# Summary-key copies on three engines instead of GpSimd, longer filler matmuls, and a new order of work in a fused attention and MLP kernel

## The chip, the cores and the metric

The kernel runs on one core of a Trainium2 chip. A core has five engines with an instruction stream each: TensorE (PE, matrix products; its weight loads are shown apart as PEld), VectorE (DVE), ScalarE (ACT), GpSimd (POOL) and SyncE (SP), which here only starts transfers (DMAs). Each engine works through its stream in order and waits at an instruction until the semaphores that it names have come. The metric is the device time of one execution in microseconds (us), less being better.

## The reference

```
scores_l = scale * q @ k^T             # only |i - j| < 16 is kept
scores_s = scale * q @ k_sum^T + log(32)
a        = softmax([scores_l, scores_s])
x        = a @ [v, v_sum]
h        = x @ w_in
out      = (h * erf(softplus(h))) @ w_out
```

q, k and v have 4 batches, 8 heads, 768 tokens and 64 features. A summary is made of each block of 32 tokens: k_sum holds the maximum of its 32 keys by feature, v_sum the mean of its values. So each head of a batch has 24 summary keys and 24 summary values. The attention's result, 3072 tokens by 512 features, goes through a gated MLP with 2048 inner features. Everything is float32.

## The kernel before

**Tiling.** The 3072 tokens are taken in six chunks of 512, the 8 heads in four pairs. A chunk and a pair make a *quad* (24 in all): scores, softmax and values for 512 tokens of two heads. A chunk's MLP is done in four groups of 512 inner features, which makes 24 *periods*. The tokens of a chunk are eight blocks of 64; each block needs the 96 keys around it (the window) and the 24 summary keys of its batch. So the tile of keys, `kw` (128 partitions x 8 blocks x 120), has 96 columns per block that a DMA brings from `k_win` (L522), and 24 that are copied from the tile `ksum` of block maxima (L527). Chunks of 512 tokens and batches of 768 don't coincide: a chunk that spans two batches has two such copies, of four blocks each, the others one of eight. Summary values stand in `vw` below 96 rows of window values.

**The first stage.** Chunk 0 takes another way. Its keys and queries (`kf` L484, `qf` L485) come whole, its values (`vt`, two transfers, L489) are summed on PE by products with a selecting matrix (L501), the result `vs` is copied to `vsum` (L504), and from there into the values' tile `vwf`: for pair 0 by an engine (L507), for pairs 1 to 3 by a DMA (L509). Window values come by L492. The weights `rw` (L313) arrive in eight parts and are converted on DVE (L330, L333, L336, then the rest by L352) and ACT (the cast, in the helper at L277). Scores are products at L565, on top of a mask (L556, L557); then row maxima on DVE (L600), the exponentials on ACT (L606), a reciprocal (L618), the normalisation (L622 on DVE or L625 on ACT), transposes on PE (L636), the copy of them on ACT (L641) and the product with the values (L662, tile `px`), which is split into `xh` (L277) and `xl` (L678) for the MLP's first product (L765, tile `h`).

**After it.** From quad 4 on, the keys of the next batch come as `rows` (L443), DVE takes the maxima (L451) and the copies at L527 bring them into `kw`. The MLP goes on with softplus (L783), erf (L884), the gate's products (L891, L896 and L903 on DVE) and the second product (L916 for the first two periods, then L920). From period 8 on, the first product is made at L806.

**What sets the order.** All work is first recorded as a list of operations with the engines that may do each and a cost for each. `P.order` then places them one after the other: it takes the engine that can start first, and on it, of the ready operations, the one with the lowest key. An operation that may go to several engines goes to the one on which it would end first. The table `TUNE` (one entry for each of 2071 operations) shifts the key, and can fix the engine. The stream of each engine is written in the order that comes out. Transfers are streamed by SP in that order too; from the ninth on, an issue is made when the transfer eight before it has landed. `FILL` names operations of PE ahead of which so many filler matmuls stand (`busy`, L959: zeros times zeros into a bank that nobody reads), and `WARM` is their number ahead of everything.

Of the kernel before, what the change touches and what calls it, by code (L numbers as in the profile page):

```python
# [26 lines left out]
NB = T // 64  # L27
NI = NB // 2
NT = T // 128
NS = 24  # L30
LW = 96
NK = LW + NS
# [7 lines left out]
WARM = 14  # L40
# [6 lines left out]
FILL = {40: 3, 51: 17, 60: 8, 90: 3, 108: 3}  # L47
# [132 lines left out]
def bfloat16(x):  # L180

    n = np.array([x], np.float32).view(np.uint32)
    return float(((n + 0x8000) & 0xFFFF0000).astype(np.uint32).view(np.float32)[0])
# [3 lines left out]
def block_attention_mlp(ctx: ExitStack, tc: tile.TileContext, q_t, k_nat, k_win, v_tok, v_nat, v_win, w_in, w_out, out):  # L187
    nc = tc.nc
# [7 lines left out]
    def sb(shape, dtype, name, tag=None):  # L196

        n = math.prod(shape[1:])
        if n % 128 == 0:
            return pool.tile(shape, dtype, name=name, tag=tag or name)  # L200
        t = pool.tile([128, -(-n // 128) * 128], dtype, name=name, tag=tag or name)[0:shape[0], 0:n]
        return t if len(shape) == 2 else t.rearrange("p (a b) -> p a b", a=shape[1]) if len(shape) == 3 else t.rearrange("p (a b c) -> p a b c", a=shape[1], b=shape[2])

    def ps(name, tag):
        return psum.tile([128, 512], F32, name=name, tag=tag)
# [5 lines left out]
    zeros = sb([128, 256], BF16, "zeros")  # L211
# [22 lines left out]
    for i in range(3):  # L234
        c = bfloat16(rest)
# [18 lines left out]
    ksum = sb([128, 2, NP, NS], F32, "ksum")  # L254
    vrows = [slice(LW, NK), slice(0, NS)]
    vsum = sb([NK, NP, 128], F32, "vsum")
# [7 lines left out]
    def pe(us, fn, r=(), w=(), **kw):  # L264
        return P.add({"PE": us}, lambda e: fn(), r, w, **kw)

    def on(us, fn, r=(), w=(), **kw):
        return P.add(us, lambda e: fn(engines[e]), r, w, **kw)

    def act(us, fn, r=(), w=(), **kw):  # L270
        return P.add({"ACT": us}, lambda e: fn(), r, w, **kw)

    def dma(kb, fn, r=(), w=(), hold=2.0, **kw):
        return P.add({"SP": max(0.45, kb / 350.0)}, lambda e: fn(), r, w, hold=hold, **kw)

    def copy(e, o, i):
        e.copy(o, i) if e is nc.scalar else e.tensor_copy(o, i)  # L277
# [194 lines left out]
    st = {}  # L472

    def where(qd):

        ch, p = divmod(qd, NP)
        seqs = {}
        for j in range(NB):
            seqs.setdefault((NB * ch + j) // SB, []).append(j)
        return ch, p, [(b, slice(js[0], js[-1] + 1)) for b, js in seqs.items()]  # L480
# [16 lines left out]
    def vsum_first(bank):  # L497
        def go(t):
            if t == 0:
                tiles[bank] = ps("vs", bank)  # L500
            nc.tensor.matmul(tiles[bank][0:NK], lhsT=pick[:, 20 - 4 * t:140 - 4 * t], rhs=vts[t // 3][:, t % 3], start=(t == 0), stop=(t == 5))  # L501
        for t in range(6):
            pe(0.87, lambda t=t: go(t), [f"vt{t // 3}"], [bank])
        act(0.5, lambda: nc.scalar.copy(vsum[LW:NK], tiles[bank][LW:NK].rearrange("s (p c) -> s p c", p=NP)), [bank], [f"vsum0{p}" for p in range(NP)])  # L504
        for p in range(NP):
            if p == 0:
                on({"POOL": 1.1}, lambda e: e.tensor_copy(st[0]["vw"][LW:NK], vsum[LW:NK, 0:1, :].to_broadcast([NS, NB, 128])), ["vsum00"], ["vwg0"])  # L507
            else:
                dma(100, lambda p=p: nc.sync.dma_start(out=st[p]["vw"][LW:NK], in_=vsum[LW:NK, p:p + 1, :].to_broadcast([NS, NB, 128])), [f"vsum0{p}"], [f"vwg{p}"])  # L509


    def load_quad(qd):
        ch, p, seqs = where(qd)
        s = st[qd] = {}

        def go_q():
            s["qb"] = sb([128, T], F32, "qb")
            nc.sync.dma_start(out=s["qb"], in_=q_t[ch, p])

        def go_k():  # L520
            s["kw"] = sb([128, NB, NK], F32, "kw")
            nc.sync.dma_start(out=s["kw"], in_=k_win[ch, p])  # L522
        dma(262, go_q, w=["qb"])
        dma(465, go_k, w=["kw"])
        for b, js in seqs:
            n = js.stop - js.start
            on({"POOL": 0.1 + 0.05 * n}, lambda e, b=b, js=js, n=n: e.tensor_copy(s["kw"][:, js, LW:NK], ksum[:, b % 2, p:p + 1, :].to_broadcast([128, n, NS])),  # L527
               [f"ksum{b % 2}{p}"], ["kw"])
# [425 lines left out]
    idle = ps("idle", "o3")  # L954

    def busy(n):

        for _ in range(n):
            nc.tensor.matmul(idle[:, 0:256], lhsT=zeros[:, 0:128], rhs=zeros, start=True, stop=True)  # L959

    busy(WARM)

    for p in range(NP):
# [6 lines left out]
    for p in range(3):  # L970
        ksum_first(p)
        scores(p, banks[p])
        softmax(p, banks[p])
    vsum_first("o2")
    ksum_first(3)
    scores(3, banks[3])
# [44 lines left out]
    def follow(n, bank=None):  # L1021
        sums(n, bank)
        load_quad(n)
        with_quad(load_nat, n + 1)
# [12 lines left out]
    for k in range(NPER):  # L1037
# [27 lines left out]
        elif k < FAST:  # L1065
# [21 lines left out]
            if qs + 1 < NQ:  # L1087
                load_quad(qs + 1)
            if qs < NQ:
                load_quad_v(qs)  # L1090
        else:
# [25 lines left out]
            if qs + 1 < NQ:  # L1117
                load_quad(qs + 1)
# [38 lines left out]
    free = {"PE": 4.15, "DVE": 1.4, "ACT": 4.2, "POOL": 5.2, "SP": 0.7}  # L1157
    plan = P.order(free, lambda n: 60 if n < 330 else 0, TUNE, "exp")
    sets = {"exp": "exp_and_others", "log": "natural_log_exp_and_others", "sig": "sigmoid_and_others", "soft": "softplus"}
    filling = True  # L1160
    for o in plan:
        if o["on"] == "PE":
            filling = filling and "o3" not in o["w"]
            if filling:
                busy(FILL.get(o["n"], 0))
        if "load" in o:
            nc.scalar.preload_act_table_set(sets[o["load"]])  # L1167
        o["fn"](o["on"])
# [40 lines left out]
```

## Time and profile before

| | |
|---|---|
| median of 3 runs | 627.41 us (626.2 to 627.84) |
| the profiled execution | 628.78 us |
| its span, first to last instruction | 627.0 us |
| mean granted clock of TensorE | 0.997 |
| PE, DVE, ACT, POOL busy | 614.3, 439.8, 412.8, 47.7 us |
| key copies on POOL (L527) | 28, 19.5 us together |
| filler matmuls on PE (L959) | 48, 7.7 us together |

A row of the profile's timeline gives start, duration, engine, line, operation, the tile written, the tile read, sizes and count; brackets at its end give the idle time of that engine ahead of it, and what ended it. A row of waits gives the total, the number of times and the longest. A row of windows gives the stretch, its length, the busy time and count of PE, PEld, DVE, ACT and POOL, the clock that TensorE was granted (1.00 is full), the share of DMA engines that were busy and the GB/s. A row of groups gives line, engine, operation, tiles and count, then the time together, the mean of one in ns, and the idle time ahead of them. Matmuls overlap, so their durations add up to more than the time from one start to the next.

### The profile page before, as it was taken

How to read it: one execution, taken by the hardware profiler on the slowest of the kernel's cores; microseconds unless marked ns; L12 is line 12 of the kernel's file. 1: busy time of each engine (PE TensorE's matmuls, PEld its weight loads, DVE VectorE, ACT ScalarE, POOL GpSimd, SP SyncE). 2: the span in 40 equal slices, each digit the busy share in tenths (PEclk: the TensorE clock that was granted, in tenths of full speed). 3: DMA queues.
4: the chain of work that ended last, by engine and by line, in shares of the span. 5: the costliest groups of instructions: out<-in, count | busy, mean ns of one | idle time of the engine just before them, and what ended most of it. 6: DMA issues, size and time to landing. Idle time of an engine off the chain costs nothing.

```text
span 627.0 us, 11997 instructions
## 1 busy us (share of the span) xinstructions
PE 614.3 (98%) x4808; PEld 517.9 (83%) x4808; DVE 439.8 (70%) x631; ACT 412.8 (66%) x822; POOL 47.7 (8%) x72
## 2 busy tenths in 40 slices
PE   7799999999999999999999999999999999999997
PEld 4685666888878889888899899898898898899886
DVE  4799999966899897768658657658657576425442
ACT  4579969977869886784585674565766555552550
POOL 2102001000442500000000000000000000000000
PEclk9899999999999999999999999999999999999999
DMA  8988867564767869899857776766597555574621
GB/s 323 266 277 333 275 214 258 190 210 149 274 190 261 313 239 363 294 326 291 289 203 246 280 265 214 247 235 216 223 292 247 197 183 192 202 264 151 253 72 67
DMA packets 36843, 150.23 MB, mean 240 GB/s; under 512 B 3956, under 2 KB 9396, under 8 KB 24244
## 3 DMA queue, kind: packets, MB, share of 16 engines
q1 hardware_dynamic: 36212, 148.95, 69.4%
q8 instruction: 38, 0.62, 0.4%
q10 hardware_dynamic: 576, 0.52, 0.3%
q14 instruction: 17, 0.14, 0.1%
HBM read 124.13 MB, written 23.07 MB: 235 GB/s over the span
## 4 chain that ended last, share of the span: by engine, by line
PE 82%; DMA 7%; ACT 5%; DVE 4%; issue 1%; SPq 1%; POOL 1%; DVEq 0%
PE ops L920 34%; PE hb L806 13%; PE h L765 11%; PE ha L806 10%; PE ops L916 4%; PE px L662 3%; DMA kf<-k_nat 2%; PE pA L565 2%; DMA out<-rows 2%; ACT L1167 2%; DMA rows<-k_nat 1%; PE pA L636 1%; PE pB L636 1%; DMA rows<-v_nat 1%; DVE a L336 1%
## 5 line engine op out<-in xcount | busy, mean ns | idle before, releaser
L920 PE MATMUL ops<-w,gh 128*128 128x512 f32 x704 | 232.1, 395 | 0.0
L920 PEld LDWEIGHTS ops<-w,gh 128*128 128x128 f32 x704 | 132.6, 188 | 27.6 <-issue 0.5
L920 PE MATMUL ops<-w,gl 128*128 128x512 f32 x352 | 137.5, 391 | 0.3 <-DVE gl L903 0.3
L1167 ACT ACT_TABLE_LOAD x86 | 110.3, 1283 | 1.5
L896 DVE TENSOR_TENSOR hc<-wt,hc 128x1024 f32<-128x1024 f32 x44 | 54.9, 1256 | 68.9 <-ACT wt L884 68.9
L765 PE MATMUL h<-xh,w 128*128 128x512 f32 x256 | 89.3, 407 | 0.0
L277 ACT COPY hc<-hb 128x256 f32<-128x256 f32 x50 | 18.6, 373 | 98.7 <-DVE hc L859 37.0
L920 PEld LDWEIGHTS ops<-w,gl 128*128 128x128 f32 x352 | 66.3, 188 | 12.7 <-DVE gl L903 0.7
L606 ACT ACTIVATE pr<-pr,stats 128x120 f32<-128x120 f32 x160 | 61.0, 383 | 7.7 <-DVE stats L615 7.5
L765 PEld LDWEIGHTS h<-xh,w 128*128 128x128 f32 x256 | 48.4, 189 | 12.7 <-issue 1.7
L806 PE MATMUL hb<-w,ws 128*128 128x256 f32 x384 | 56.5, 283 | 0.8 <-DVE hc L277 0.8
L903 DVE TENSOR_TENSOR gl<-hc,gh 128x1024 fp32r<-128x1024 f32 x44 | 54.8, 1244 | 2.0 <-ACT gh L277 1.1
L806 PEld LDWEIGHTS hb<-w,ws 128*128 128x128 f32 x384 | 50.7, 192 | 1.0 <-DVE hc L277 1.0
L884 ACT ACTIVATE wt<-wt 128x1024 f32<-128x1024 f32 x48 | 50.6, 1062 | 0.4
L765 PE MATMUL h<-xl,w 128*128 128x512 f32 x128 | 50.2, 392 | 0.0
L527 POOL COPY kw<-ksum 128x96 f32<-128x96 f32 (+1 forms) x28 | 19.5, 710 | 391.1 <-DMA kw<-k_win 278.3
L277 DVE CAST gh<-hc 128x1024 fp32r<-128x1024 f32 x39 | 28.2, 724 | 15.8 <-PE ops L920 14.2
L872 ACT ACTIVATE wt<-hc 128x1024 f32<-128x1024 f32 x32 | 32.2, 1051 | 0.2
L277 DVE COPY hc<-hb 128x256 f32<-128x256 f32 x46 | 19.4, 423 | 16.4 <-PE hb L806 15.3
L856 DVE TENSOR_TENSOR hc<-hb,hc 128x256 f32<-128x256 f32 x32 | 13.5, 422 | 23.8 <-PE hb L806 22.0
L606 ACT ACTIVATION_READ_ACCUMULATOR pr<-pr,stats 128x1 f32 x160 | 30.0, 187 | 0.0
L916 PE MATMUL ops<-a32s,gw 128*128 128x512 f32 x64 | 29.4, 596 | 0.0
(163 smaller groups left out, 1084.1 us busy)
## 6 DMA issues: line engine op xcount, KB each, us to landing
w<-dr SPq DMA_DIRECT2D x36, 1024.0 KB, 6.8
ws<-ds SPq DMA_DIRECT2D x30, 1024.0 KB, 8.1
kw<-k_win SPq DMA_DIRECT2D x20, 480.0 KB, 5.3
rw<-w_in SPq DMA_DIRECT2D x8, 1024.0 KB, 7.4
rw<-w_out SPq DMA_DIRECT2D x8, 1024.0 KB, 5.2
dr<-w SPq DMA_DIRECT2D x8, 1024.0 KB
ds<-ws SPq DMA_DIRECT2D x8, 1024.0 KB, 6.6
vw<-v_win SPq DMA_DIRECT2D x20, 384.0 KB, 5.2
```

The source lines that it names most:

```text
L277: e.copy(o, i) if e is nc.scalar else e.tensor_copy(o, i)
L527: on({"POOL": 0.1 + 0.05 * n}, lambda e, b=b, js=js, n=n: e.tensor_copy(s["kw"][:, js, LW:NK], ksum[:, b % 2, p:p + 1, :].to_broadcast([12 ...
L606: nc.scalar.activation(s["pr"][:, j], s["pr"][:, j] if qd >= MQ else s["sc"][j // NI][:, i * NK:(i + 1) * NK], AF.Exp, scale=0.125, bias=s ...
L765: nc.tensor.matmul(hs[k, f][:, 0:T], lhsT=w[m], rhs=xt[ch, cc][x], start=(cc == 0 and n == 0), stop=(cc == 3 and n == 2))
L806: nc.tensor.matmul(shape, lhsT=w[m], rhs=y[l], start=first and c == 0 and i == 0, stop=c == 1 and i == 2, skip_group_check=True)
L872: nc.scalar.activation(wt[k, n], hc[k, n], AF.Softplus)
L884: act(0.96, lambda n=n: nc.scalar.activation(wt[k, n], wt[k, n], AF.Erf, scale=-1.0 if k < SOFT else 1.0), [s], [s], table=("sig",), after ...
L896: e.tensor_tensor(hc[k, n], wt.pop((k, n)), hc[k, n], op=ALU.mult)
L903: e.tensor_tensor(gs[k, n][1], hc.pop((k, n)), f32(gs[k, n][0]), op=ALU.subtract)
L916: nc.tensor.matmul(os_[ch, t], lhsT=x[0][:, i % 2, t * 128:(t + 1) * 128], rhs=w32["o", g, i // 2][:, i % 2], start=first, stop=last)
L920: nc.tensor.matmul(os_[ch, t], lhsT=x[y][:, i % 2, t * 128:(t + 1) * 128], rhs=w[m], start=first and n == 0, stop=last and n == 2)
L1167: nc.scalar.preload_act_table_set(sets[o["load"]])
```

## The change

The two copies may now go to three engines, by a helper that issues the copy of whichever engine is chosen; GpSimd's cost in the planner is raised. A filler matmul has 512 columns instead of 256; their number falls from 48 to 33, at other places. The table `TUNE` is a new one throughout (three of its entries are shown).

```
-WARM = 14
+WARM = 7
...
-TUNE = {0: (-3981.299057, 1.5, 0, None), 1: (-3981.726255, 1.5, 0, None), 2: (-3976.161371, 1.5, 0, None), ...
-FILL = {40: 3, 51: 17, 60: 8, 90: 3, 108: 3}
+TUNE = {0: (-4728.546832, 1.5, 0, None), 1: (-4728.985158, 1.5, 0, None), 2: (-4669.297502, 1.5, 0, None), ...
+FILL = {30: 10, 40: 3, 60: 6, 89: 2, 91: 1, 101: 1, 110: 2, 111: 1}
...
             if p == 0:
-                on({"POOL": 1.1}, lambda e: e.tensor_copy(st[0]["vw"][LW:NK], vsum[LW:NK, 0:1, :].to_broadcast([NS, NB, 128])), ["vsum00"], ["vwg0"])
+                on({"POOL": 1.35, "DVE": 1.13, "ACT": 0.95}, lambda e: copy(e, st[0]["vw"][LW:NK], vsum[LW:NK, 0:1, :].to_broadcast([NS, NB, 128])), ["vsum00"], ["vwg0"])
...
-            on({"POOL": 0.1 + 0.05 * n}, lambda e, b=b, js=js, n=n: e.tensor_copy(s["kw"][:, js, LW:NK], ksum[:, b % 2, p:p + 1, :].to_broadcast([128, n, NS])),
+            on({"POOL": 0.5 + 0.05 * n, "DVE": 0.06 + 0.025 * n, "ACT": 0.2 + 0.018 * n}, lambda e, b=b, js=js, n=n: copy(e, s["kw"][:, js, LW:NK], ksum[:, b % 2, p:p + 1, :].to_broadcast([128, n, NS])),
...
     def busy(n):
...
-            nc.tensor.matmul(idle[:, 0:256], lhsT=zeros[:, 0:128], rhs=zeros, start=True, stop=True)
+            nc.tensor.matmul(idle.rearrange("q (n c) -> q n c", n=2), lhsT=zeros[:, 0:128], rhs=zeros.unsqueeze(1).to_broadcast([128, 2, 256]), start=True, stop=True)
```

What becomes of it in the streams is shown at three places. A copy by the helper stands at L277, whichever engine makes it. The first place is the head of SP's stream, the first transfers of the program (vt: values of chunk 0; kf, qf: its keys and queries; rw: weights). Before:

```order
L484 DMA kf<-k_nat 128x768
L485 DMA qf<-q_t 128x512
L489 DMA vt<-v_tok 128x3x512
L313 DMA rw<-w_in 128x2048
L489 DMA vt<-v_tok 128x3x512
L484 DMA kf<-k_nat 128x768
L485 DMA qf<-q_t 128x512 x3
L484 DMA kf<-k_nat 128x768
L492 DMA vwf<-v_win 96x1024
L484 DMA kf<-k_nat 128x768
```

And now:

```order
L485 DMA qf<-q_t 128x512
L484 DMA kf<-k_nat 128x768
L489 DMA vt<-v_tok 128x3x512 x2
L484 DMA kf<-k_nat 128x768
L313 DMA rw<-w_in 128x2048
L485 DMA qf<-q_t 128x512 x3
L484 DMA kf<-k_nat 128x768
L492 DMA vwf<-v_win 96x1024
L484 DMA kf<-k_nat 128x768
```

The second transfer of values and the second of keys have gone ahead of the first part of the weights; the third transfer of keys has the same transfers ahead of it as before. On PE the six products of L501, three before and three behind 17 fillers, now stand together, with ten fillers behind them.

The second place is ACT's stream ahead of the first softplus of the MLP (L783), where h of the first period is copied and the keys of quad 4, the second chunk's first, are made ready. Before:

```order
L641 COPY ptr<-pA 120x512
L641 COPY ptr<-pB 120x512
L277 CAST xh<-px 128x512
L277 CAST w<-a_592 128x1024
L277 COPY hc<-h 128x512 x2
L1167 ACT_TABLE_LOAD
L783 ACTIVATE wt<-hc 128x1024
```

And now:

```order
L641 COPY ptr<-pA 120x512
L641 COPY ptr<-pB 120x512
L277 CAST xh<-px 128x512
L277 CAST w<-a_584 128x1024
L277 COPY hc<-h 128x512
L277 COPY kw<-ksum 128x4x24
L277 COPY hc<-h 128x512
L1167 ACT_TABLE_LOAD
L783 ACTIVATE wt<-hc 128x1024
```

One of quad 4's two key copies, that for the four blocks of batch 0, has come in between the two copies of h. The other, for the four blocks of batch 1, needs the maxima of L451. It stands first of the key copies in GpSimd's stream, which the difference of the two streams behind the constants shows:

```order
-L507 COPY vwf<-vsum 24x1024
-L527 COPY kw<-ksum 128x4x24 x8
-L527 COPY kw<-ksum 128x8x24 x3
+L277 COPY vwf<-vsum 24x1024
+L277 COPY kw<-ksum 128x4x24 x4
+L277 COPY kw<-ksum 128x8x24
 L394 TENSOR_TENSOR sums<-w 128x2x256 x4
```

The copy of the first values has stayed on GpSimd (L507 is L277 now), and seven of 28 key copies have, five of them ahead of the sums of L394; of the others twelve are on ACT and nine on DVE. On DVE, L451 is followed by L333, L352 and L336 as before, and then by a copy of h.

2 lines of the change are left out of this document (1 added, 1 removed).

## The prediction

> **What bounds the kernel now.** I read the page first, then the waits of the engine that is busiest, then those stretches of its timeline in which it waits.
>
> ```profile
> span 627.0 us, 11997 instructions
> PE 614.3 (98%) x4808; PEld 517.9 (83%) x4808; DVE 439.8 (70%) x631; ACT 412.8 (66%) x822; POOL 47.7 (8%) x72
> PE   7799999999999999999999999999999999999997
> PEclk9899999999999999999999999999999999999999
> ```
>
> PE is busy for 614.3 of 627.0 us, and of the 40 slices only the first two and the last lie below 9. So a change that leaves the products as they are can win only what PE loses to waits, to filler matmuls and to a halved clock. The waits of PE, longest first (total, times, longest):
>
> ```profile
> PE vs L501 <- DMA vt<-v_tok: 2.2, 1, 2.2
> PE h L565 <- issue: 2.1, 1, 2.1
> PE pA L565 <- POOL kw L527: 1.6, 1, 1.6
> PE o L565 <- DMA kf<-k_nat: 1.1, 1, 1.1
> PE idle L959 <- DVE zeros L212: 1.1, 1, 1.1
> PE hb L806 <- DVE hc L277: 0.8, 1, 0.8
> PE ops L920 <- DVE gl L903: 0.3, 1, 0.3
> ```
>
> One of the seven is for a copy of summary keys: 1.6 us. The last two (1.1 us) are all that PE waits after 52 us, up to its last product, so everything else lies in the first stage, where the timeline of PE (start, duration, count, idle before) shows it:
>
> ```profile
> 9.35 2.81 PE L501 MATMUL vs<-vt,pick 128*120 128x512 f32 x6 [2.22 <-DMA vt<-v_tok]
> 11.99 2.02 PE L959 MATMUL idle<-zeros 128*128 128x256 bf16 x17
> 13.85 2.80 PE L501 MATMUL vs<-vt,pick 128*120 128x512 f32 x6
> 18.85 0.49 PE L959 MATMUL idle<-zeros 128*128 128x256 bf16 x3
> 20.45 0.97 PE L565 MATMUL o<-kf,qf 64*64 64x16 f32 x36 [1.11 <-DMA kf<-k_nat]
> 23.18 1.05 PE L959 MATMUL idle<-zeros 128*128 128x256 bf16 x8
> 27.73 0.30 PE L565 MATMUL h<-kf,qf 64*64 64x96 f32 x2 [2.11 <-issue]
> 34.44 0.49 PE L959 MATMUL idle<-zeros 128*128 128x256 bf16 x3
> 50.51 0.31 PE L565 MATMUL pA<-kw,qb 64*64 64x120 f32 x1 [1.56 <-POOL kw L527]
> 51.08 0.50 PE L765 MATMUL h<-xh,w 128*128 128x512 f32 x1
> 56.68 3.59 PE L916 MATMUL ops<-a32s,gw 128*128 128x512 f32 x8
> ```
>
> A filler takes (13.85 - 11.99) / 17 = 0.109 us. The 2.11 us pause waits for no data. The transfers of 25 to 26 us contain one packet of instructions, and I read the pause as PE running out of code while its next block stands behind data:
>
> ```profile
> q8 instruction: 1, 0.02, 7.4%
> 24.56:27.97 3.41, 1.30 (x51) 1.03 (x52) 1.89 (x3) 2.91 (x17) 0.00 (x0) 1.00 1.01 344
> 27.97:31.38 3.41, 3.41 (x43) 3.23 (x37) 2.60 (x7) 1.03 (x3) 0.00 (x0) 0.50 1.05 223
> 7.49:10.90 3.41, 1.55 (x4) 0.83 (x5) 0.50 (x2) 2.78 (x16) 0.00 (x0) 1.00 1.01 374
> ```
>
> The last three rows are stretches of 3.41 us (first PE, last but two the granted clock). After the one with 1.30 us of PE work the clock is 0.50 for the whole next one, which costs half of it, 1.7 us. The one with 1.55 us of work had no such follower (the page's second slice, 15.7 to 31.4 us, is the only one after the first below 9 tenths). So a point between 1.30 and 1.55 us of work decides here. The Trainium skill, "TensorE: Matmul & The Clock Gate", Part 1, says that the clock drops after an idle window of about 3.4 us; by that rule a pause of 2.1 us inside a window would cost nothing, and then the term for the clock below would be no gain of the change at all. The row with 0.50 contradicts it here, and the measurement decides.
>
> What really sets the start of the second quad's chain is not PE but VectorE and GpSimd:
>
> ```profile
> 28.78 1.22 DVE L600 TENSOR_REDUCE stats<-h 128x4 f32<-128x480 f32 x2 [2.29 <-PE h L565]
> 33.64 0.69 DVE L277 CAST xh<-px 128x512 fp32r<-128x512 f32 x1 [0.56 <-PE px L662]
> 45.99 0.94 DVE L451 TENSOR_REDUCE ksum<-rows 128x24 f32<-128x768 f32 x1
> 46.85 1.21 DVE L333 SCALAR_TENSOR_TENSOR a32s<-rw,a32s 128x1024 uint32<-128x1024 uint32 x1
> 49.12 1.22 DVE L336 SCALAR_TENSOR_TENSOR a32s<-rw,a32s 128x1024 uint32<-128x1024 uint32 x1
> 45.00 0.26 POOL L527 COPY kw<-ksum 128x96 f32<-128x96 f32 x1 [25.69 <-DVE a L336]
> 46.99 3.47 POOL L527 COPY kw<-ksum 128x96 f32<-128x96 f32 x1 [1.73 <-DVE ksum L451]
> ```
>
> DVE has no gap from 28.78 on but the 0.56 us before 33.64. Then L451 makes the maxima, and the copy of them, which took 0.26 us when alone, takes 3.47 us: it ends at 50.46, just after the last of the three weight conversions of DVE (L333, L352, L336) that began with it. PE starts 0.05 us later. So the first-stage pause of PE pushes DVE, and DVE pushes that copy and PE.
>
> **The change part by part.** *The copies.* Of 28 key copies twelve go to ACT, nine to DVE, and seven stay on GpSimd, among them the one that PE waits for. The copy of the first values stays there too. Their prices come from these groups (busy, mean ns, idle before; in the row of k_win issues, KB each and us to landing; the last two rows are of the timeline):
>
> ```profile
> L527 POOL COPY kw<-ksum 128x96 f32<-128x96 f32 (+1 forms) x28 | 19.5, 710 | 391.1 <-DMA kw<-k_win 278.3
> L277 ACT COPY hc<-hb 128x256 f32<-128x256 f32 x50 | 18.6, 373 | 98.7 <-DVE hc L859 37.0
> L277 DVE COPY hc<-hb 128x256 f32<-128x256 f32 x46 | 19.4, 423 | 16.4 <-PE hb L806 15.3
> kw<-k_win SPq DMA_DIRECT2D x20, 480.0 KB, 5.3
> 36.94 2.40 ACT L625 ACTIVATE prf<-prf,stats 128x120 f32<-128x120 f32 x8 [0.39 <-DVE stats L618]
> 30.79 1.15 DVE L622 TENSOR_TENSOR prf<-prf,stats 128x960 f32<-128x960 f32 x1
> ```
>
> No row shows such a copy on ACT or DVE. Below, it is free; above, it takes the 128x256 copy's 0.37 and 0.42 us; it writes 96 or 192 elements a row, so I take 0.3 us. Twelve on ACT make 3.6 us and nine on DVE at most 2.7 us over 627 us, on engines that are idle for 214 and 187 us: nothing on PE's path, with 12 x 0.37 + 9 x 0.42 = 8.2 us as the other end. One of the twelve stands between two copies of h ahead of the first softplus, +0.3 us there. One normalisation of the first pair also goes from DVE to ACT, ahead of the first value sums' copy; it is done long before PE's wait for kf at 20.45 ends, and that wait hides it (cover gone: 2.40 - 1.15 = 1.25 us).
>
> *The wait at 48.95 to 50.51.* The copy stays behind L451 with L333, L352 and L336 beside it in the changed order as well, so its 3.47 us stay. The Trainium skill, "GPSIMD Engine Reference", section 1 (Specifications), says that GpSimd shares its SBUF interfaces with VectorE and contends with its instructions that have two SBUF inputs; the two rows of 0.26 and 3.47 us agree. If that rule is the whole story, this wait stays as long as the copy stays on GpSimd. What moves is DVE's clock time: it begins with the scores of the fourth first-stage pair, whose end I work out next.
>
> *Values sums and fillers to 20.45.* The second v_tok transfer now goes ahead of the first weights (and the second keys too). All six products of L501 (two passes each) can run on from 9.35, to about 14.6, then ten fillers of 512 columns. At twice the columns I take twice the time, 0.218 us: 2.2 us, to 16.8 instead of 16.58. The following three fillers add 0.3 us. Both vanish in the wait for kf, which held PE until 20.45 and should still: as many bytes stand ahead of that transfer. If the cover went, it would be 0.5 us. The warm-up (7 of 512 for 14 of 256) is the same work.
>
> *Fillers and code, 20.45 to 28.8.* Six long fillers for eight short ones: 1.31 - 0.87 = +0.43 us. The shorter code (32 instructions fewer up to there) puts the end of the block some 16 products later, and the new block comes when it came: so the pause begins later and ends at about 27.7 as before. I estimate a pause of 1.7 us, between 0 and 2.11. More of the 34 + 34 products are done by then, and those scores end at 28.2 instead of 28.78: -0.5 us. The stretch 24.56 to 27.97 then holds 3.41 - 1.7 = 1.7 us of work, over the 1.55 that kept the clock: -1.7 us on PE (0 if it drops again).
>
> *Fillers 28.8 to 48.* Seven long for six short ones: 1.53 - 0.50 = +1.0 us on PE. (In the 34.44 row the three took 0.25 us up to the next row.) All this is PE's time, which isn't the bound here: it arrived at the second quad's other half at 48.95 and waited until 50.51.
>
> *The sum.* DVE starts 0.5 us earlier, and its gap of 0.56 us goes with the full clock: its chain and the copy end 1.1 us earlier, 50.46 - 1.1 = 49.4. PE, ahead of that: 48.95 with +0.43 - 0.41 - 1.7 + 1.03 = 48.3, and with three more L765 products (51 instead of 48 stand ahead) 49.0. It waits 0.4 us instead of 1.56. The 24 products from 51.08 to 56.68 take 0.23 us each, and 21 are left: first output product at 49.4 + 0.6 + 21 x 0.23 = 54.8 instead of 56.68, **-1.9 us**. The first output product needs the gate product L891 of VectorE; from ACT's rows moved by the same 1.1 us and 0.3 us for the copy I put its end at 54.1, with 0.7 us to spare. From 230 us on the order of PE is that of before; between 57 and 230 us PE is full, so 1.9 us stay. The profiled execution took 628.78 us (its span 627.0), which gives 626.9; but it was 1.4 us over the median of the three runs, so I take the sum from the median: 627.41 - 1.9 = **625.5 us**.
>
> **The rivals.** *Nothing changes.* Fillers only fill, the pause comes at the same length, the clock halves again: then DVE's chain moves by nothing, and the three products more (0.7 us) stand against 1.0 us of fillers: 626.9 to 627.4. For it: the three runs of before spread by 1.6 us, about one halved stretch, so the median may hold none. Against: the two v_tok and the three moved products are in the order. That the change doesn't do what it says belongs here too: the copy that PE waits for stays on GpSimd.
>
> *Slower: a copy stops an in-order engine.* On GpSimd a key copy waited for its transfer (278.3 us in all, in 13 waits) with nothing behind it. On ACT and DVE the softplus, erf, exponentials and gate products stand behind it. The place is 50 to 125 us, where DVE is full:
>
> ```profile
> 80.00:100.00 20.00, 20.00 (x127) 12.50 (x127) 20.00 (x26) 14.25 (x31) 1.32 (x2) 1.00 0.72 240
> ```
>
> Price: the wait less the slack, which is 0.7 us by the sum above. ACT and DVE take over four key copies in that stretch; the keys land 5.3 us after their issue, so a copy that is due 2 us before its landing costs 1.3 us. It decides from the second such copy on (2.6 us, over the 1.9 us of gain); three make 625.5 + 3.9 = 629.4.
>
> *Faster: the pause goes.* If the code block comes in time, DVE starts 2.1 us earlier instead of 0.5: 625.5 - 1.6 = 623.9.
>
> **How the numbers follow.** About 0.3% (1.9 us) is what a measurement of this kernel can tell from no change. Forecast, 624.4 to 626.2: 0.48, of it 0.32 below 625.5, since the two later waits (1.1 us) may go as well, and 0.16 above. Pause gone, 622.5 to 624.4: 0.12. No change, 626.2 to 629.3: 0.22. Slower, 629.3 to 633: 0.18. So faster 0.32 + 0.12 = 0.44, same 0.16 + 0.22 = 0.38, slower 0.18. The range that leaves out two tenths, 0.16 above and 0.04 below, is 623.0 to 629.6; it holds both ends of the pause and of the clock (0 to 2.1 and 0 to 1.7 us), and of the dearer copies what isn't hidden by idle engines.
>
> **What would show it.** The v_tok rows together from 9.35 on; a pause of PE that waits for "issue" near 26 us and under 2.1 us, with clock 1.00 behind it; the GpSimd copy still at about 3.5 us, ending near 49.4; first L916 near 54.8. Wrong it would be with a clock of 0.5 after 28 us, or with rows of ACT or DVE that wait for k_win after 52 us and PE waiting behind them.

## The result, and the profile after

| | before | changed |
|---|---|---|
| median | 626.81 us (4 runs, 625.98 to 627.84) | 631.21 us (4 runs, 630.52 to 632.63) |
| profiled execution, its span | 628.78, 627.0 us | 630.62, 628.8 us |
| ratio | | 1.0072, interval 1.0046 to 1.0099 |

The changed kernel is slower by 0.7%, where 625.5 us were forecast and the range ended at 629.6. One run below, of the version with the key copy on DVE and short fillers, was a slow one (862.4 us at a granted clock of 0.66, and the one that was traced) and isn't counted. The page of the changed kernel, in the lines that were shown of before:

```profile
span 628.8 us, 11970 instructions
PE 617.0 (98%) x4793; PEld 515.8 (82%) x4793; DVE 436.9 (69%) x636; ACT 418.5 (67%) x845; POOL 42.9 (7%) x51
PEclk9999999999999899999999999999999999999999
```

The slice with a lower clock has moved from the second (near 28 us) to the fourteenth (204 to 220 us). The waits of PE (total, times, longest) name what is there:

```profile
PE pA L636 <- DVE pr L622: 2.1, 1, 2.1
PE vs L501 <- DMA vt<-v_tok: 1.7, 1, 1.7
PE idle L959 <- DVE zeros L212: 1.1, 1, 1.1
PE h L565 <- issue: 1.0, 1, 1.0
PE o L565 <- DVE ksum L495: 0.8, 1, 0.8
PE h L565 <- DMA qf<-q_t: 0.7, 1, 0.7
PE pA L565 <- POOL kw L277: 0.6, 1, 0.6
PE ops L920 <- DMA w<-dr: 0.2, 1, 0.2
```

The first row is new: the transposes of a softmax (the twelfth quad's) wait 2.1 us for its normalisation on DVE. The first stage went nearly as forecast. In PE's timeline:

```profile
9.03 5.38 PE L501 MATMUL vs<-vt,pick 128*120 128x512 f32 x12 [1.69 <-DMA vt<-v_tok]
27.98 0.53 PE L565 MATMUL h<-ksum,qf 64*64 64x24 f32 x19 [1.00 <-issue]
49.56 0.31 PE L565 MATMUL pA<-kw,qb 64*64 64x120 f32 x1 [0.63 <-POOL kw L277]
55.03 2.73 PE L916 MATMUL ops<-a32s,gw 128*128 128x512 f32 x6
```

The first output product stands at 55.03 us, 1.65 us earlier than in the trace of before (56.68). To follow where that lead went I compared the two traces by work done (the products done by a time, each at its line's usual spacing, fillers at nothing): the lead is between 1.2 and 1.7 us at nearly every mark from 70 to 210 us, and from 230 us on the changed kernel is 2 to 3 us behind. PE, DVE and GpSimd there, in the timeline of the changed kernel:

```profile
212.84 0.39 PE L765 MATMUL h<-xh,w 128*128 128x512 f32 x1
215.35 0.63 PE L636 MATMUL pA<-ident,pr 128*120 128x128 f32 x4 [2.12 <-DVE pr L622]
203.86 1.35 DVE L277 COPY kw<-ksum 128x192 f32<-128x192 f32 x1
210.15 0.68 DVE L277 CAST gh<-hc 128x1024 fp32r<-128x1024 f32 x1
210.75 0.19 DVE L618 RECIPROCAL stats<-stats 128x8 f32<-128x8 f32 x1
210.87 2.19 DVE L903 TENSOR_TENSOR gl<-hc,gh 128x1024 fp32r<-128x1024 f32 x1
212.98 2.22 DVE L622 TENSOR_TENSOR pr<-pr,stats 128x960 f32<-128x960 f32 x1
202.87 5.97 POOL L394 TENSOR_TENSOR sums<-w 128x512 f32<-128x512 f32 x4 [22.51 <-DVE stats L615]
208.92 1.29 POOL L397 TENSOR_TENSOR sums<-sums 128x512 f32<-128x512 f32 x1
210.29 1.69 POOL L397 TENSOR_TENSOR sums<-sums 128x512 f32<-128x512 f32 x1
212.05 2.14 POOL L397 TENSOR_TENSOR sums<-sums 128x512 f32<-128x512 f32 x1
214.27 2.08 POOL L397 TENSOR_TENSOR sums<-sums 128x512 f32<-128x512 f32 x1
```

And the same operations in the timeline of before:

```profile
213.08 1.23 DVE L903 TENSOR_TENSOR gl<-hc,gh 128x1024 fp32r<-128x1024 f32 x1
215.08 1.15 DVE L622 TENSOR_TENSOR pr<-pr,stats 128x960 f32<-128x960 f32 x1
207.00 5.42 POOL L397 TENSOR_TENSOR sums<-sums 128x512 f32<-128x512 f32 x4
218.12 0.60 PE L636 MATMUL pA<-ident,pr 128*120 128x128 f32 x4
```

Before, GpSimd's sums of weights were over at 212.4, L903 and L622 took 1.23 and 1.15 us, and PE came for the result 1.9 us after it was done. Now the new order starts the sums later and calls for the transposes five microseconds earlier. L903 and L622 stand beside the sums, take 2.19 and 2.22 us, and PE, free at 213.2, gets the result at 215.2.

The single sums tell how the two engines slow each other. The second sum ends at 211.98, L903 1.08 us after it, the third sum 1.13 us after that, L622 1.01 us after that, and the fourth sum 1.15 us after that. By itself a sum takes 1.29 us, L903 1.23 and L622 1.15. So by these rows neither engine runs at half speed: they take turns, and each row of 2.1 to 2.2 us is a wait for the other engine's operation and then about the usual duration.

The windows of the changed kernel show what follows:

```profile
212.93:216.34 3.41, 1.29 (x11) 1.02 (x10) 3.41 (x4) 1.16 (x2) 3.33 (x2) 1.00 0.98 351
216.34:219.75 3.41, 3.41 (x10) 2.63 (x9) 1.59 (x2) 2.81 (x5) 0.01 (x1) 0.50 0.63 207
```

PE is busy for 1.29 of 3.41 us, and the next 3.41 us are granted half the clock: 1.7 us more. **Theory A**: it is these two, 2.1 + 1.7 = 3.8 us, and their cause is that DVE's two-input operations and GpSimd's sums hold each other up. The rivals: B, key copies on in-order engines block what stands behind them; C, the trace had a disturbed stretch; D, the new order puts the normalisation too late even without the contention.

### The profile page after: what moved, and what is told of

Same layout as the page of the kernel before. It is cut to its first block, busy times and chain, and to the rows that moved or that the text cites. A ratio compares the mean times of both kernels' runs of the same rounds, so it can differ in the third digit from the quotient of the medians.

```text
span 628.8 us, 11970 instructions
## 1 busy us (share of the span) xinstructions
PE 617.0 (98%) x4793; PEld 515.8 (82%) x4793; DVE 436.9 (69%) x636; ACT 418.5 (67%) x845; POOL 42.9 (7%) x51
## 4 chain that ended last, share of the span: by engine, by line
PE 88%; DVE 5%; DMA 3%; ACT 1%; issue 1%; POOL 1%; SPq 0%; POOLq 0%; DVEq 0%
PE ops L920 38%; PE hb L806 14%; PE ha L806 11%; PE h L765 11%; PE ops L916 4%; PE px L662 3%; PE pA L565 3%; DMA rw<-w_in 2%; PE pA L636 1%; PE pB L636 1%; DMA w<-dr 1%; DVE a L333 1%; DVE a L336 1%; POOL kw L277 1%; ACT L1167 0%
## 5 line engine op out<-in xcount | busy, mean ns | idle before, releaser
L896 DVE TENSOR_TENSOR hc<-wt,hc 128x1024 f32<-128x1024 f32 x44 | 53.6, 1226 | 73.5 <-ACT wt L884 73.4
L765 PE MATMUL h<-xh,w 128*128 128x512 f32 x256 | 93.8, 419 | 0.0
L277 ACT COPY hc<-hb 128x256 f32<-128x256 f32 x52 | 19.4, 373 | 85.1 <-DVE hc L859 34.5
L903 DVE TENSOR_TENSOR gl<-hc,gh 128x1024 fp32r<-128x1024 f32 x44 | 55.2, 1256 | 2.6 <-ACT gh L277 1.8
L277 DVE CAST gh<-hc 128x1024 fp32r<-128x1024 f32 x39 | 28.0, 717 | 14.5 <-PE ops L920 13.3
L765 PEld LDWEIGHTS h<-xl,w 128*128 128x128 f32 x128 | 24.4, 191 | 6.4 <-issue 1.9
L277 DVE COPY hc<-hb 128x256 f32<-128x256 f32 x44 | 18.6, 423 | 15.7 <-PE hb L806 15.0
```

The source lines that it names most:

```text
L765: nc.tensor.matmul(hs[k, f][:, 0:T], lhsT=w[m], rhs=xt[ch, cc][x], start=(cc == 0 and n == 0), stop=(cc == 3 and n == 2))
L896: e.tensor_tensor(hc[k, n], wt.pop((k, n)), hc[k, n], op=ALU.mult)
L903: e.tensor_tensor(gs[k, n][1], hc.pop((k, n)), f32(gs[k, n][0]), op=ALU.subtract)
```

## The experiments

Each version is the changed kernel, or before, with the edit shown; the order that the planner makes is kept but for that. `move(n, m)` takes operation n out of the common order and puts it ahead of m; the streams of the other engines stay.

**The changed kernel again.**

> The changed kernel itself, for a second trace and a narrower interval on the same chip as the next three. Theory A (DVE runs a two-input multiplication and subtraction at half speed beside GpSimd's sums near 211 us, so that one normalisation, L622, ends 2.1 us late, PE waits for it, and the halved clock behind that wait costs 1.7 us): the wait of about 2.1 us at the 12th quad's transposes is there again, L903 and L622 near 2.2 us, and the time is 3 to 5 us above before. Rival B (copies of keys on in-order engines block what is behind them): waits of ACT or DVE for k_win with PE waiting behind them. Rival C (only chance: the first trace had a disturbed stretch): no wait at that place, and the time within 2 us of before.

Median 630.56 us beside 627.56 for 35 runs of before: ratio 1.0053 (1.0030 to 1.0077). The second trace has the wait again, L903 at 2.19 and L622 at 2.22 us:

```profile
PE h L565 <- issue: 2.4, 1, 2.4
PE pA L636 <- DVE pr L622: 2.1, 1, 2.1
```

C is out. The mean clock that each run reports counts halved stretches: one takes 1.7 of some 627 us, 0.0027. Of these 12 runs of the changed kernel eleven are at 0.995 or lower (about two stretches or more), of its first four two; of 99 runs of before, from here and the two sets below, 20 are.

**The normalisation ahead of the product split.** Operation 661 is L622 of the twelfth quad, 728 the L903 that stood ahead of it.

```
     plan = P.order(free, lambda n: 60 if n < 330 else 0, TUNE, "exp")
+    move(661, 728)
```

> As the changed kernel, but that one normalisation (L622 of the 12th quad) goes ahead of the product split L903 on DVE. Sums on GpSimd stay beside it. Theory A: L622 still takes about 2.2 us, but starts at 210.9 and ends at 213.1, before PE asks for it at 213.2; no wait of 2.1 us, no half clock behind it: 3.8 us less than the changed kernel (span about 625). Rival B: no difference. Rival C: no difference.

Median 627.17 us, ratio to before 0.9988 (0.9964 to 1.0012): 3.4 us less than the changed kernel. The swapped version's timeline still has the contention, but no wait of PE for it:

```profile
209.65 2.02 DVE L622 TENSOR_TENSOR pr<-pr,stats 128x960 f32<-128x960 f32 x1
211.59 2.30 DVE L903 TENSOR_TENSOR gl<-hc,gh 128x1024 fp32r<-128x1024 f32 x1
211.81 0.62 PE L636 MATMUL pA<-ident,pr 128*120 128x128 f32 x4
```

L622 ends 0.14 us ahead of the transposes. Two of its 12 runs are at 0.995 or lower. So the loss is the wait at this place with what follows it; whether contention or order made it late is for the next one.

**Smaller sums on GpSimd.** Four of the sums take 16 of their 128 columns; the rest of those sums is left out.

```
         def plus(e, o, x, y, op):
-            e.tensor_tensor(s["t"][:, :, o], s["t"][:, :, x], s["t"][:, :, y], op=op)
+            c = slice(0, 16) if g == 3 else slice(0, 128)
+            e.tensor_tensor(s["t"][:, :, o, :, c], s["t"][:, :, x, :, c], s["t"][:, :, y, :, c], op=op)
```

> As the changed kernel in every stream, but the four second-stage sums (L397) of the second set of weights on GpSimd take 16 of 128 columns, so that part of the weights' sums is left out. They end before 211 us. Theory A, contention: L903 and L622 at that place take 1.23 and 1.16 us instead of 2.2, the wait of PE and the half clock go: about 3.8 us less than the changed kernel. Rival D (the new order alone puts that normalisation too late): L903 and L622 may get shorter, but PE still waits there for over 1 us, and the time is that of the changed kernel within 1 us. Rival B: no difference.

Median 626.76 us, ratio 0.9982 (0.9964 to 1.0001): 3.8 us less than the changed kernel, with the order of every stream as it was. Its timeline (lines are one higher from L397 on):

```profile
211.14 1.23 DVE L904 TENSOR_TENSOR gl<-hc,gh 128x1024 fp32r<-128x1024 f32 x1
212.29 1.27 DVE L623 TENSOR_TENSOR pr<-pr,stats 128x960 f32<-128x960 f32 x1
209.61 0.33 POOL L398 TENSOR_TENSOR sums<-sums 128x64 f32<-128x64 f32 x1
211.37 1.19 POOL L398 TENSOR_TENSOR sums<-sums 128x64 f32<-128x64 f32 x1
213.74 0.60 PE L637 MATMUL pA<-ident,pr 128*120 128x128 f32 x4
```

The durations are near those of before (1.23 and 1.15 us), the normalisation is done at 213.56, and PE, which comes at 213.74, doesn't wait there. D falls: the order is in time, by 0.18 us, if DVE isn't held up. I had expected the small sums to end before 211; the last ended at 212.56. It is the one that was held up: the first took 0.33 us, the last started 0.23 us after L904 and took 1.19. So the turns are taken here too, but a short sum leaves DVE little to wait for; other sizes weren't tried.

**Fillers into the wait.** Eight products of 512 columns into the bank that the transposes overwrite.

```
             s["tp"] = [ps(n, n) for n in PA]
+            if qd == 11:
+                for _ in range(8):
+                    nc.tensor.matmul(s["tp"][0].rearrange("q (n c) -> q n c", n=2), lhsT=zeros[:, 0:128], rhs=zeros.unsqueeze(1).to_broadcast([128, 2, 256]), start=True, stop=True)
```

> As the changed kernel, but eight filler products of 512 columns (about 1.75 us) stand ahead of the 12th quad's transposes, into the bank that the transposes write afterwards. Theory A: the normalisation is as late as before, the wait shrinks to 0.4 us, but PE is busy in that stretch, so the clock stays full behind it: about 1.7 us less than the changed kernel. If the clock halves for another reason than PE's idle time, the time stays.

Median 629.53 us, ratio to before 1.0023 (1.0001 to 1.0046): 1.0 us less than the changed kernel by the medians and 1.9 by the ratios, where 1.7 were expected, with no run at 0.995 or lower. Its timeline:

```profile
213.74 1.90 PE L636 MATMUL pA<-zeros 128*128 128x512 bf16 x8
216.05 0.62 PE L639 MATMUL pA<-ident,pr 128*120 128x128 f32 x4 [0.41 <-DVE pr L622]
213.67 2.23 DVE L622 TENSOR_TENSOR pr<-pr,stats 128x960 f32<-128x960 f32 x1
```

And the windows, the stretch behind the wait:

```profile
216.25:219.66 3.41, 3.41 (x20) 2.77 (x18) 2.11 (x3) 2.88 (x5) 0.79 (x1) 1.00 0.81 291
```

The normalisation is as late, the wait is filled, and the clock stays at 1.00 behind it. So the half clock follows from PE's idle time there. A loss of about 2 us (629.53 beside 627.56) remains, as large as the wait of 2.1 us that the fillers stand in for.

**The copies.** In one version all 28 key copies are on GpSimd again, on top of the swap; in the other before's own order has the 21 copies on ACT and DVE. The former:

```
+    for o in plan:
+        if o["n"] in ACT + DVE:
+            o["on"] = "POOL"
```

The latter, with the copies going through the changed kernel's helper, and with `ACT` and `DVE` in both versions the lists of the twelve and nine operations that the change moved (not printed):

```
+    for o in plan:
+        if o["n"] in ACT + DVE:
+            o["on"] = "ACT" if o["n"] in ACT else "DVE"
```

> The swapped version (L622 of the 12th quad ahead of L903), with all 28 key copies on GpSimd as before the change; each at the place in the common order where it stood. Theory A (the copies are worth nothing either way): within 1 us of the swapped version, 627.2 us; no wait on a key copy but that near 49 us, 0.5 to 1.6 us. Rival B (copies on ACT and DVE cost time by blocking): 1 to 3 us less than the swapped version. Rival E (they are what the change gains by): 1 to 3 us more.

> The kernel before, in its own order and with its own fillers, but with the 21 key copies on ACT and DVE that the change puts there, at the places where they stood. Theory A: the time of before within 1 us, and no wait of PE that ends with such a copy. Rival B: rows of ACT and DVE that wait for k_win, PE waiting behind them, 2 to 4 us more than before.

Beside 628.43 us of before on this chip: 628.48 us, ratio 1.0019 (0.9998 to 1.0041), and 627.67 us, ratio 0.9994 (0.9971 to 1.0018). The second is before within the interval, so moving the copies costs nothing that could be told, at most 0.2% by the interval. The first is 1.3 us above the swapped version by its median, more than the 1 us that I had allowed, but on another chip; by the ratios the difference is 0.3% with an uncertainty as large. It isn't below it, as B had it. Whether the copies gain anything (rival E) stays open. Before with the new copies has the waits of ACT, but no row of PE behind them, and B falls; its waits for k_win:

```profile
POOL kw L277 <- DMA kw<-k_win: 89.8, 4, 43.9
ACT kw L277 <- DMA kw<-k_win: 5.3, 2, 4.8
```

**The one copy that PE waits for.** Operation 186 goes to DVE, right behind the maxima, ahead of L333 (130), with the swap.

```
+    move(661, 728)
+    move(186, 130)
+    for o in plan:
+        if o["n"] == 186:
+            o["on"] = "DVE"
```

> The swapped version, with the one key copy that PE waits for near 49 us (second half of the first quad of chunk 1) on DVE right behind the maxima of L451 instead of on GpSimd. Theory A: it takes 0.2 to 0.3 us and is done near 47.2 us, so PE's wait of 0.6 to 0.7 us there goes and the time falls by 0.5 to 0.7 us, unless the first gate product (L891) becomes the bound, which had 0.7 us to spare by my sum: then 0 to 0.3 us. Rival F (that copy's 3.4 us is GpSimd's own price and not contention) gives the same; the contention is told by the rows of the other copies.

> The version with the swap and the key copy on DVE once more, to narrow its interval: ratio to before between 0.996 and 1.000; no wait of PE near 49 us and none at the 12th quad's transposes.

627.04 us, ratio 0.9983 (0.9957 to 1.0009), and in the second set 627.81 us, ratio 1.0011 (0.9987 to 1.0035), above the 0.996 to 1.000 that I had expected. The wait near 49 us is gone in both traces, and the copy's price is told by the first:

```profile
43.58 0.21 DVE L277 COPY kw<-ksum 128x96 f32<-128x96 f32 x1
51.87 2.81 PE L916 MATMUL ops<-a32s,gw 128*128 128x512 f32 x6
```

0.21 us instead of 3.4. Rival F, that 3.4 us is GpSimd's own price, is out by a row that was shown of before: there a copy of the same size took 0.26 us on GpSimd, at 45.00. The first output product at 51.87 us is the earliest of all traces, and that run had a span of 622.5 us. The second trace of the same kernel has it at 56.87, 5 us later: there the pause for instructions was 2.3 us and the clock halved twice.

```profile
23.97:27.38 3.41, 1.35 (x52) 1.07 (x50) 1.83 (x3) 2.79 (x17) 0.00 (x0) 1.00 1.01 287
27.38:30.79 3.41, 3.13 (x29) 2.91 (x29) 2.42 (x7) 0.95 (x2) 0.00 (x0) 0.50 1.01 240
30.79:34.20 3.41, 3.41 (x23) 2.37 (x23) 1.88 (x2) 2.97 (x17) 0.00 (x0) 0.50 1.02 238
```

So the wait is gone, and the expected 0.5 to 0.7 us can't be told from the scatter.

**Short fillers**, alone with the swap, and with the key copy on DVE.

```
-            nc.tensor.matmul(idle.rearrange("q (n c) -> q n c", n=2), lhsT=zeros[:, 0:128], rhs=zeros.unsqueeze(1).to_broadcast([128, 2, 256]), start=True, stop=True)
+            nc.tensor.matmul(idle[:, 0:256], lhsT=zeros[:, 0:128], rhs=zeros, start=True, stop=True)
```

> The swapped version, with fillers of 256 instead of 512 columns in the same numbers (33). Theory A (fillers before 20 us are hidden by the wait for keys, those behind it cost PE time that mostly stands in front of a wait on DVE and GpSimd): warm-up ends earlier, so PE starts cold for longer, but with data at 9 us; after 20 us 13 fillers save up to 1.4 us of PE, of which 0 to 0.5 us remain at the first output product; the mean clock over the runs falls by up to 0.002, since less work stands beside the pause for instructions. Together within 1 us of the swapped version. Rival G (long fillers are what holds the clock): 1.5 to 2.5 us more, mean clock lower by 0.003 or more.

> The version with the swap and the key copy on DVE, with fillers of 256 columns. Theory A: as that version within 1 us; if the time that fillers take on PE is now the bound up to the first output product, up to 1 us less.

627.61 us, ratio 0.9980 (0.9960 to 0.9999), with the clock of the swapped version over its runs (0.998 both): G falls. With the key copy on DVE the other eleven runs have a median of 627.10 us, ratio 0.9991 (0.9968 to 1.0013).

**Everything but the order.** This is before's order with the 21 copies on ACT and DVE, as above, and with the change's fillers of 512 columns at its places.

```
-WARM = 14
+WARM = 7
-FILL = {40: 3, 51: 17, 60: 8, 90: 3, 108: 3}
+FILL = {30: 10, 40: 3, 60: 6, 89: 2, 91: 1, 101: 1, 110: 2, 111: 1}
```

> The kernel before in its own order, with the 21 key copies on ACT and DVE and with the change's fillers (512 columns, its numbers and places): everything of the change but the new order. Theory A: no wait at the 12th quad's transposes, 626.5 to 629 us, so the loss of the change is the order's alone. If copies and fillers together cost something, the 3 us of the changed kernel are there.

629.00 us, ratio 1.0022 (1.0000 to 1.0044), with no wait at the twelfth quad. The long fillers in the old order may cost up to 0.4%. Most of it stands near 20 us in its trace: the three fillers ahead of the products of 20.45 us start at 20.98 us, where before has them at 18.85, behind a second wait of 1.6 us for v_tok. That wait isn't in the changed kernel, whose loss is at another place.

**Before again**, for a second trace of its first stage.

> The kernel before, once more, for a second trace of its first stage. If the first trace's start of 56.7 us for the first output product (L916) hung on the halved clock behind the pause for instructions, a trace without it has that start near 55 us and a span near 625 us, which is where the changed kernel stood at that point; if the halved stretch is there again, 56.5 us or later and a span of 626 to 628 us.

One run: 628.76 us, span 627.0, first output product at 56.93 us. The clock was full behind the pause for instructions, but halved from 50.29 us on, behind the wait for the key copy (1.6 us there too), as the windows show:

```profile
46.88:50.29 3.41, 1.82 (x35) 1.31 (x35) 2.47 (x3) 3.36 (x4) 2.24 (x1) 1.00 0.95 377
50.29:53.70 3.41, 3.41 (x9) 2.63 (x8) 3.41 (x6) 3.37 (x5) 0.00 (x0) 0.50 0.87 341
```

Neither of the two cases that I had written down came true. It settles another thing: the wait of 0.8 us near 291 us that the first trace of before had, and that seemed to be gained by the change, isn't in this one.

No version is shown to beat before. Of those that compute the whole result the best ratios are 0.9980, whose interval ends at 0.9999 and which was run in one set only, the lowest of ten ratios, and 0.9983, which came out at 1.0011 when run again.

## Why the prediction was wrong

The sum put the changed kernel 1.9 us below before. **The step that failed is "between 57 and 230 us PE is full, so 1.9 us stay".** I had only read there that PE had no wait in the old order; in the new order it has one, shown by two traces, and taken away by two edits at that place alone (3.4 and 3.8 us less). Its terms are 2.1 us for the wait and 1.7 us for the half clock behind it. The step takes it for granted that a normalisation is as ready in the new order as in the old, and the prediction prices no operation of DVE there. In the old order L903 and L622 of this quad come behind the sums on GpSimd (1.23 and 1.15 us), in the new one beside them (2.19 and 2.22 us). I had used this very contention, in the row where a GpSimd copy took 3.47 instead of 0.26 us, and looked at one side of it only. The other side's price stood in the trace of before, where another L903 is beside the first set of sums:

```profile
171.51 2.18 DVE L903 TENSOR_TENSOR gl<-hc,gh 128x1024 fp32r<-128x1024 f32 x1
170.89 1.72 POOL L394 TENSOR_TENSOR sums<-w 128x512 f32<-128x512 f32 x1
172.69 2.15 POOL L397 TENSOR_TENSOR sums<-sums 128x512 f32<-128x512 f32 x1
```

The Trainium skill's sentence that I cited ("GPSIMD Engine Reference", section 1) puts the contention down to DVE's instructions with two SBUF inputs or in a 2-port perf mode, and doesn't say what either side loses. L903 and L622 have two such inputs. Operations with one input are hit as well: the key copy at 203.86, beside the sums, took 1.35 us, where one of its size took 0.25 us in the trace of before with the copies moved; no run here shows in which mode it ran. The cast at 210.15 took its usual 0.68 us, but it came between two sums, and the sum that started beside it took 1.69 us.

Point by point:

- **Sums of values and fillers to 20.45 us.** The two transfers came as expected: all six products from 9.03 on in one row. A wait for queries (0.7 us) and one for the maxima of L495 (0.8 us) were new and not foreseen. The products that were to wait for kf until 20.45 started at 20.46, but that was luck: there is no wait for kf, PE was busy up to then, and the fillers that this wait was to hide are not hidden by it.
- **Pause and clock.** I put the pause at 1.7 us; it was 1.0 in the first trace of the changed kernel, with full clock behind it. But in six traces with the change's own first stage (the changed kernel twice, the swap, the small sums, the filled wait, the copies on GpSimd) it was 1.0 to 2.4 us, and the clock halved behind it in three. The term of 1.7 us for the clock was no property of the change: before's first trace happened to have a halved stretch there. That the pause is one for code fits all 14 traces: in each PE goes on 1.3 to 1.7 us after a packet of instructions has landed (in before's it lands at 26.29 us, and PE goes on at 27.73).
- **DVE's chain and the key copy.** Forecast to end at 49.4, it ended at 49.50; PE waited 0.63 us, 0.4 were forecast; the first output product at 55.03, 54.8 were forecast. The mechanism was right, the gain too large: before's order has that product at 56.68, 56.93 and (with the copies moved) 54.94, mean 56.2; those six traces have 55.03, 55.41, 53.66, 55.64, 55.68 and 55.14, mean 55.1. That is 1.1 us by nine traces that scatter over 3 us, not 1.9. Before's order with the change's fillers, at 58.20, isn't among them.
- **The copies** cost PE nothing that shows, as said. Mostly the size was right too: 0.25 us on DVE and 0.27 on ACT by the median in the changed kernel's trace, 0.3 were taken. The exception is the one of 1.35 us beside the sums.
- **The rivals.** The slower one gave 629.4 us and was near by its time, but for a mechanism that isn't there: ACT and DVE wait for k_win, and nobody waits for them. The slower case had 0.18, and none of the rivals was the contention.

The new sum: -1.1 + 2.1 + 1.7 = 2.7 us, beside 3.3 us measured in the larger set (1.9 to 4.8 by its interval) and 4.5 in the first (2.9 to 6.2). What is left I can't assign: waits of 0.2 to 1.5 us for weights (w<-dr) near 245 us come in several traces, in one of before too.

## What to carry to other kernels

Where an order is made by planned durations, look for pairs of engines that hold each other up, and reckon an operation's slack with the longer duration: about 1 us more on each of two operations ate a slack that was 1.9 us in the old order and, by the version with the small sums, 0.2 us in the new one. That duration can stand in a trace of the old order already, at another place. A wait of 2 us on an engine that is otherwise full can cost nearly twice that, if its clock falls behind it. And a gain read from two single traces is worth only as much as the first stage's scatter from run to run: take several before a term of the sum is built on a pause or a halved stretch.

## What the runs showed of the hardware

- DVE's two-input operations and GpSimd's two-input sums hold each other up: L903 went from 1.23 to 2.19 us, L622 from 1.15 to 2.22 us, and L397 on GpSimd from a median of 1.30 to 1.88 us each. By the starts and ends of the rows they take turns. With an eighth of the columns on GpSimd, DVE took 1.23 and 1.27 us, and the last short sum 1.19 instead of 0.33 us.
- It isn't two inputs alone: a one-input copy on DVE took 1.35 instead of 0.25 us beside the sums.
- The point that I had put between 1.30 and 1.55 us of PE work in 3.41 us doesn't hold as one number: 1.29, 1.30 and 1.35 us were followed by half the clock, 1.55 was not, but 1.82 in the second trace of before was.
- Over 99 runs of before, those at a mean clock of 1.000 (18) took 626.1 us on average, those at 0.997 (43) 627.7, those at 0.994 and 0.995 (18) 629.9: the mean clock, that is the number of halved stretches, accounts for about half of the variance of these runs (0.52).
